# Block 1's row statistics on ScalarE, two turned quarters copied by VectorE, chunk 2's scores in one PE run, and a new order table, in an attention-plus-ReGLU layer

## The chip, the core and the metric

The kernel runs on one core of a Trainium2 chip. The metric is device microseconds of one execution, lower is better. The core has a matrix engine (TensorE; PE in the profile, with PEld for its weight loads), VectorE (DVE), ScalarE (ACT), GpSimd (POOL) and SyncE (SP). Each takes its instructions in the order in which the program lists them, and waits for the others by semaphores. SP, ACT and POOL also issue DMAs.

## The reference

Input x is 2048 rows of 512 values in bfloat16. An attention block and a gated linear block follow each other, both on normalised rows, both added to what came in:

```python
def _layernorm(x, axis=-1, eps=1e-5):
    m = jnp.mean(x, axis=axis, keepdims=True)
    v = jnp.var(x, axis=axis, keepdims=True)
    return (x - m) / jnp.sqrt(v + eps)
...
    qkv = (x @ wqkv)                     # 32 heads of 16
    idx = pos[:, None] - (arange(8) * 2) # each row sees itself and 7 rows before, 2 apart
    logits = einsum("bhsd,bhswd->bhsw", q, kg) * scale   # masked where idx < 0
    o = einsum("bhsw,bhswd->bhsd", softmax(logits), vg)
    h = x + o @ wo
...
    gate, up = n @ W_gate, n @ W_up      # n = _layernorm(h), F = 1376
    h2 = h + (gate * (gate > 0) * up) @ W_down
```

## The kernel before

The 2048 rows are worked in four chunks (tk = 0 to 3) of 512 rows, and a chunk has four blocks of 128 rows (j = 0 to 3), one row to a partition. A chunk goes through these steps:

- **Normalise x** (`layernorm`, from line 453). For a block j, VectorE makes mean and variance (BN_STATS at L488, BN_AGGR at L491), ScalarE makes 1/sqrt(var + eps) as exp(-0.5 ln(var + eps)) (L504 and L508), and the block is scaled: in chunk 0 by VectorE (L539), in chunks 1 to 3 by ScalarE (L536), which needs a small VectorE product for its bias first (nb, L512). Chunk 0 does this block by block (`XG[0]` has four groups), the others in one group of four.
- **Turn** the rows, so that features lie on partitions: PE transposes (L568) into a PSUM bank, which is copied to SBUF (L584); the fourth chunk's x and the rows of the second half are turned by DMA (L557). In chunk 0 each block is a quarter of the turned tile `quad`, with a copy of its own.
- **q, k, v** (PE L609, copied out by ScalarE at L617). In chunk 0 the first outputs are made in parts: a half-width part "a" over quarters 0 and 1, a half-width part "b" over quarters 2 and 3, then full-width parts.
- **Scores** in two halves of four neighbours each: VectorE multiplies q by shifted k (L675 in chunk 0, L660 later), PE sums over the head by a matrix of ones (`sel`, four 32-column strips side by side). In the halves named by `PRE` VectorE first adds the two products (L704), and PE's run is 8 matmuls (L718) in place of 16 (L666). ScalarE takes exp (L746). `MS = (3,)` names the chunks in which both halves' score matmuls stand in one PE run.
- **Softmax and values**: sum and reciprocal (L763, L769, L772), DMAs that spread the weights over partitions (L806), VectorE products with shifted v (L853 in chunk 0, L838 later), sums partly by accumulating DMAs (L881), output projection (PE L919), residual and row sum (DVE L930).
- **Gated block**: normalise h, turn it, gate and up (PE L996), their last 96 columns (PE L959), relu and copies on ScalarE (L1001, L1003, L1006), product on VectorE (L1027), down projection (PE L1050), and the output row (DVE L1058 in chunks 2 and 3).

The program is written by a planner. Every step is an `Op` with an engine, an estimated cost and its dependencies; `RANK` gives each one a place. `Plan.order` takes the steps strictly in the order of RANK, gives each a planned start and a buffer, and the steps are then emitted by planned start. On one engine that is the order of RANK. The estimated costs decide which buffer of a pool a step gets, and nothing else of the result.

The names that the change touches are settings ahead of `layernorm`: `MS`, `TEV` (quarters of chunk 0 whose turned copy VectorE makes), `XS` (where ScalarE makes the row statistics of x) and `RANK`. The steps it touches run through these lines:

```python
groups = XG[tk]
xnT, xev, _, _ = layernorm(tk, xload[tk], xnT_s, lnp, groups, LNA[0][tk])
...
tev = not residual and tk == 0 and j0 in TEV
if tev: V.tensor_copy(out=o, in_=i)
else:   nc.scalar.copy(out=o, in_=i)
```

Of the kernel before, what the change touches and what calls it, by code (L numbers as in the profile page):

```python
# [201 lines left out]
def kernel(  # L202
# [187 lines left out]
    BDI = {"S": 0.63, "A": 0.65, "P": 0.95}  # L390

    RPE, POW = (), ()

    MERGE = (0, 1, 2, 3)

    MS = (3,)

    BCN = 4

    HG = ([[0, 1, 2, 3]],) * 4  # L400
    HSP = ()
    XG = ([[0], [1], [2], [3]], [[0, 1, 2, 3]], [[0, 1, 2, 3]], [[0, 1, 2, 3]])
# [737 lines left out]
```

## Time and profile before

| | |
|---|---|
| median of 3 runs | 191.66 us (191.09 to 192.36) |
| the profiled execution | 191.45 us |
| span inside it | 189.7 us, so 1.75 us lie around the span |
| PE busy | 183.7 us, 97% |
| VectorE busy | 148.9 us, 79% |
| ScalarE busy | 117.2 us, 62% |
| GpSimd busy | 25.1 us, 13% |

All sums are made against the 191.45 us of the profiled execution, whose trace is the one shown; it lies 0.21 us under the median. Times in the rows count from the start of the span. A merged row of the timeline shows start, length, engine, line, operation, tiles written and read, and the count; in brackets stands how long the engine had been idle before it, and what ended that. Matmuls are pipelined: a row's length holds the tail of its last one, so the pace of PE is read from starts, not from the lengths of single matmuls.

### The profile page before, as it was taken

Reading aid. Unit: us, or ns where it says so; the run is one execution under the profiler, and the core shown is the slowest. Engines: PE = TensorE matmul, PEld = TensorE weight load, DVE = VectorE, ACT = ScalarE, POOL = GpSimd, SP = SyncE. Lnnn points to the kernel's source line nnn. Section 1 sums busy time; section 2 is a strip of 40 time slices with the busy share of each in tenths; the row PEclk is TensorE's granted clock in tenths of the full one; section 3 lists DMA queues with packets and bytes.
Section 4 is the critical chain, followed back from the end, with each engine's and each line's share of the span. In section 5 each row is a group of like instructions: output and inputs, shape, how many; then the busy total and the mean of one; then the engine's idle time right before and its main releaser. Section 6 shows DMA issues by size and latency. Waiting matters only on the chain.

```text
span 189.7 us, 2952 instructions
## 1 busy us (share of the span) xinstructions
PE 183.7 (97%) x1058; PEld 93.3 (49%) x1077; DVE 148.9 (79%) x226; ACT 117.2 (62%) x239; POOL 25.1 (13%) x47
## 2 busy tenths in 40 slices
PE   7799999999999999999999999999999999999994
PEld 7655455554444444544444554455444444455543
DVE  5799989999999999999999997999473720115343
ACT  2769999986496867925477783047465702659600
POOL 4000311500000024040031351013300000000000
PEclk9999999999999999999999999999999999999999
DMA  6999294992497869943564999666970150200313
GB/s 170 294 321 386 52 215 88 198 198 47 146 242 166 246 179 188 201 77 107 109 133 83 194 181 196 141 128 143 194 133 3 28 138 0 83 3 28 100 54 95
DMA packets 27742, 26.96 MB, mean 142 GB/s; under 512 B 14704, under 2 KB 23248, under 8 KB 27728
## 3 DMA queue, kind: packets, MB, share of 16 engines
q1 hardware_dynamic: 23552, 15.21, 29.3%
q0 software_dynamic: 3312, 10.49, 29.1%
q10 hardware_dynamic: 864, 1.08, 1.8%
q8 instruction: 8, 0.13, 0.3%
q14 instruction: 6, 0.05, 0.1%
HBM read 8.42 MB, written 2.10 MB: 55 GB/s over the span
## 4 chain that ended last, share of the span: by engine, by line
PE 79%; DVE 7%; DMA 7%; ACT 3%; issue 2%; POOL 0%; DVEq 0%
PE bank L996 36%; PE bank L1050 20%; PE bank L609 10%; PE bank L919 7%; DMA x_sm<-in_A_x_dram 4%; DVE big L675 4%; PE bank L959 3%; DMA big<-ex 3%; DVE st L488 2%; ACT row L536 2%; PE bank L666 2%; PE bank L718 1%; DVE big L853 1%; ACT quad L617 1%; POOL big L806 0%
## 5 line engine op out<-in xcount | busy, mean ns | idle before, releaser
L996 PE MATMUL bank<-quad,wgu_sb 128*128 128x512 bf16 x312 | 71.4, 379 | 0.4
L996 PEld LDWEIGHTS <-wgu_sb 128*128 128x128 bf16 x320 | 31.0, 98 | 36.9 <-issue 1.3
L1050 PE MATMUL bank<-wd_sb,gT 128*128 128x512 bf16 (+4 forms) x193 | 39.3, 355 | 0.3
L1006 ACT ACTIVATE gr<-bank 128x512 bf16<-128x512 f32 x40 | 22.9, 600 | 12.1 <-PE bank L996 7.4
L609 PE MATMUL bank<-quad,wqk_sb 128*128 128x512 bf16 (+1 forms) x130 | 29.6, 370 | 0.6 <-ACT quad L584 0.4
L1050 PEld LDWEIGHTS <-gT 128*128 128x128 bf16 (+1 forms) x198 | 18.5, 98 | 19.6
L1003 ACT CAST up_sb<-bank 128x512 bf16<-128x512 f32 x30 | 17.3, 588 | 16.5 <-PE bank L996 14.3
L1027 DVE TENSOR_TENSOR gT<-gr,up_sb 128x1024 bf16<-128x1024 bf16 x20 | 13.6, 688 | 14.8 <-ACT up_sb L1003 10.0
L660 DVE TENSOR_TENSOR big<-quad,kT 128x4096 bf16<-128x4096 bf16 x11 | 25.0, 2287 | 0.0
L609 PEld LDWEIGHTS <-wqk_sb 128*128 128x128 bf16 x134 | 14.8, 114 | 13.4 <-issue 1.9
L838 DVE TENSOR_TENSOR big<-big,vT 128x4096 bf16<-128x4096 bf16 x9 | 20.2, 2288 | 0.0
L609 PE MATMUL bank<-quad,wv_sb 128*128 128x512 bf16 x62 | 15.5, 379 | 0.1
L930 DVE SCALAR_TENSOR_TENSOR x_sm<-x_sm,bank 128x512 bf16<-128x512 bf16 x16 | 10.7, 680 | 5.6 <-PE bank L919 5.6
L1058 DVE SCALAR_TENSOR_TENSOR row<-bank,iv,x_sm 128x512 bf16<-128x512 f32 (+2 forms) x10 | 6.2, 641 | 11.3 <-ACT iv L508 7.8
L478 ACT ACTIVATE junk<-x_sm,sm 128x512 bf16<-128x512 bf16 x16 | 11.5, 724 | 5.7 <-DVE x_sm L930 5.7
L919 PE MATMUL bank<-wo_sb,quad 128*128 128x512 bf16 x64 | 15.0, 379 | 0.0
L1056 ACT ACTIVATE up_sb<-bank,iv 128x512 bf16<-128x512 f32 x8 | 5.3, 685 | 13.2 <-PE bank L1050 13.2
L881 POOL DMA_DIRECT2D big<-big x12 | 10.5, 878 | 21.6 <-DVE big L838 11.5
L841 DVE TENSOR_TENSOR big<-big 128x1024 bf16<-128x1024 bf16 (+2 forms) x18 | 11.7, 661 | 0.7 <-DMA big<-big 0.6
L488 DVE BATCH_NORM_STATS2 st<-x_sm 128x6 f32<-128x512 bf16 x16 | 10.4, 676 | 1.9 <-DMA x_sm<-in_A_x_dram 1.9
L617 ACT CAST kT<-bank 128x512 bf16<-128x512 f32 x16 | 9.1, 594 | 3.0 <-PE bank L609 3.0
L806 POOL DMA_DIRECT2D big<-ex x12 | 6.8, 591 | 26.9 <-DVE st L488 19.4
(80 smaller groups left out, 188.0 us busy)
## 6 DMA issues: line engine op xcount, KB each, us to landing
big<-big POOLq DMA_DIRECT2D x12, 512.0 KB, 5.5
big<-ex SPq DMA_DIRECT2D x20, 128.0 KB, 2.8
big<-ex POOLq DMA_DIRECT2D x12, 128.0 KB, 4.5
wqk_sb<-wqk_sb POOLq DMA_DIRECT2D x3, 512.0 KB, 5.5
wgu_sb<-in_B_W_gate_dram SPq DMA_DIRECT2D x1, 1376.0 KB, 10.4
wgu_sb<-in_B_W_up_dram SPq DMA_DIRECT2D x2, 688.0 KB, 4.9
wd_sb<-in_B_W_down_dram SPq DMA_DIRECT2D x2, 640.0 KB, 5.5
x_sm<-in_A_x_dram SPq DMA_DIRECT2D x2, 512.0 KB, 6.3
```

The source lines that it names most:

```text
L478: nc.scalar.activation(out=junk[:, j % 2, :], in_=h.t[:] if h else x_sm[:, tk * BPC + j, :], func=ACT.Square, bias=sm.t[:, j:j + 1], scale ...
L488: V.bn_stats(out=st.t[:], in_=x_sm[:, tk * BPC + j, :])
L609: nc.tensor.matmul(mm.t[:, lo:hi], lhsT=wv_sb[:, dt, t:D:NT] if c == 2 else wqk_sb[:, dt, c * D + t:(c + 1) * D:NT], rhs=xnT.t[:, dt, lo:h ...
L660: V.tensor_tensor(out=pb.t[:].rearrange("p (t w) s -> p t w s", t=2), in0=q4, in1=k4, op=ALU.mult)
L838: V.tensor_tensor(out=mt.t[:], in0=ab.t[:], in1=v8, op=ALU.mult)
L841: V.tensor_tensor(out=mt.t[:, 0:n, :], in0=mt.t[:, 0:n, :], in1=mt.t[:, n:2 * n, :], op=ALU.add)
L919: nc.tensor.matmul(od.t[:], lhsT=OT.t[:, t, j * P:(j + 1) * P], rhs=wo_sb[:, t, :], start=(t == 0), stop=(t == NT - 1 and tk not in RPE))
L996: nc.tensor.matmul(mm.t[:fs, lo:hi], lhsT=wgu_sb[:, dt, g, ft * P: ft * P + fs], rhs=hnT.t[:, dt, lo:hi], start=(dt == 0), stop=(dt == NT ...
L1003: nc.scalar.copy(out=ub.t[:fs, i, :], in_=um.t[:fs, :])
L1006: nc.scalar.activation(out=gr.t[:fs, i, :], in_=gm.t[:fs, :], func=ACT.Relu, scale=-1.0 if tk in HX else 1.0)
L1027: V.tensor_tensor(out=gt.t[:fs, 0:n, :], in0=gr.t[:fs, 0:n, :], in1=ub.t[:fs, 0:n, :], op=ALU.mult)
L1050: nc.tensor.matmul(od.t[:, c0:c1], lhsT=gts[ft].t[:fs, ft % 2, j * P:(j + 1) * P], rhs=wd_sb[:fs, ft, c0:c1], start=(ft == 0), stop=(ft == ...
```

## The change

The settings change in four places:

- `XS = ((0, 1),)`: in chunk 0 the statistics of block 1 are made by ScalarE. A Copy activation with scale -1/512 sums the row (its accumulator gives minus the mean), and a Square activation with that as bias sums the squared deviations. The setting now names pairs of chunk and group, where it named chunks. The block is then scaled on VectorE by (x + minus mean) times the reciprocal root.
- `TEV = (2, 3)`: the turned copies of quarters 2 and 3 of chunk 0 are made by VectorE.
- `MS = (2, 3)`: chunk 2's two score halves stand in one PE run, too.
- `RANK` is another table, so all engines get another order, and buffers change places. One estimated cost (the issue of chunk 0's first half of spreading DMAs on GpSimd) is 0.85 in place of 0.35.

New branches for the bias product (`f_na`, `f_n1`, `XNA`) are not reached with these settings. The arithmetic of all other steps stays as it was. Lines from 480 on move down by 6 to 16: L568 is L584 after the change, L584 is L598 (VectorE) and L600 (ScalarE), L609 is L625, L666 is L682, L718 is L734.

```diff
 RANK = [
-    1, 0, 3, 2, 4, 6, 7, 8, 9, 10, 15, 11, 16, 17, 18, 19, 20, 21, 5, 12,
...
+    1, 0, 3, 2, 6, 8, 11, 10, 15, 16, 13, 12, 17, 14, 18, 19, 20, 21, 4, 7,
...
-    MS = (3,)
+    MS = (2, 3)
...
-    TEV = ()
+    TEV = (2, 3)
     HX = (0,)
-    XS = ()
+    XS = ((0, 1),)
+    XNA = ()
...
-        own = not residual and tk in XS
-        sm, sq = (residual, Buf(sq_s)) if residual else (Buf(sm_s), Buf(sq_s)) if own else (None, None)
+        has = not residual and [g for g in groups if (tk, g[0]) in XS]
+        sm, sq = (residual, Buf(sq_s)) if residual else (Buf(sm_s), Buf(sq_s)) if has else (None, None)
...
+            own = not residual and (tk, grp[0]) in XS
...
                             nc.scalar.activation(out=junk[:, j % 2, :], in_=x_sm[:, tk * BPC + j, :],
-                                                 func=ACT.Copy, accum_out=sm.t[:, j:j + 1])
+                                                 func=ACT.Copy, scale=-1.0 / D, accum_out=sm.t[:, j:j + 1])
...
-                                             bias=sm.t[:, j:j + 1], scale=-float(D), accum_out=sq.t[:, j:j + 1])
+                                             bias=sm.t[:, j:j + 1], scale=1.0 if own else -float(D), accum_out=sq.t[:, j:j + 1])
...
                 elif own:
                     nc.scalar.activation(out=rs.t[:, lo:hi], in_=sq.t[:, lo:hi], func=ACT.Ln,
-                                         bias=eps_t[:, 0:1], scale=float(D) ** -3)
+                                         bias=eps_t[:, 0:1], scale=1.0 / D)
...
+                elif own:
+                    V.tensor_scalar(out=xn.t[:], in0=x, scalar1=sm.t[:, j:j + 1], scalar2=rs.t[:, j:j + 1], op0=ALU.add, op1=ALU.mult)
```

**ScalarE at the start of the program, before**: after the table load come the four pairs of Ln (L504) and Exp (L508) for the reciprocal roots `rs` of blocks 1, 0, 3 and 2, then the four copies of turned quarters, then the first q and k copies. `mv` holds VectorE's mean and variance.

```order
L328 ACT_TABLE_LOAD
L504 ACTIVATE rs0_131<-mv0_117,eps_t_66 128x1
L508 ACTIVATE rs0_131<-rs0_131 128x1
L504 ACTIVATE rs0_131<-mv0_117,eps_t_66 128x1 x2
L508 ACTIVATE rs0_131<-rs0_131 128x1 x2
L584 COPY quad0_79<-bank1_141 128x4x128
L584 COPY quad0_79<-bank2_142 128x4x128
L584 COPY quad0_79<-bank3_143 128x4x128
L584 COPY quad0_79<-bank4_144 128x4x128
L617 CAST kT_77<-bank1_141 128x512
```

**The same place after the change**: `sm` is minus the mean of block 1, `sq` its squared deviations. In the program's operands the Ln steps are of blocks 1, 0, 3 and 2, the Exp steps of blocks 0, 1, 3 and 2.

```order
L328 ACT_TABLE_LOAD
L478 ACTIVATE junk_139,sm0_121<-x_sm_71 128x512
L484 ACTIVATE junk_139,sq0_124<-x_sm_71,sm0_121 128x512
L507 ACTIVATE rs0_131<-sq0_124,eps_t_66 128x1
L510 ACTIVATE rs0_131<-mv0_117,eps_t_66 128x1
L514 ACTIVATE rs0_131<-rs0_131 128x1
L510 ACTIVATE rs0_131<-mv0_117,eps_t_66 128x1
L514 ACTIVATE rs0_131<-rs0_131 128x1 x2
L600 COPY quad0_79<-bank1_141 128x4x128
L600 COPY quad0_79<-bank2_142 128x4x128
L633 CAST kT_77<-bank5_145 128x512
```

Two full-row activations now stand ahead of every reciprocal root, and two of the four copies are gone from this queue.

**VectorE at the same place, before**: four blocks' statistics are done ahead of the four scaled blocks (`row0` to `row3`), and behind those stand the statistics of chunk 1.

```order
L488 BN_STATS st3_116<-x_sm_71 128x6
L491 BN_AGGR mv0_117<-st2_115 128x2
L491 BN_AGGR mv0_117<-st3_116 128x2
L539 TENSOR_SCALAR row0_104<-x_sm_71,mv0_117,rs0_131 128x512
L539 TENSOR_SCALAR row1_105<-x_sm_71,mv0_117,rs0_131 128x512
L539 TENSOR_SCALAR row2_106<-x_sm_71,mv0_117,rs0_131 128x512
L539 TENSOR_SCALAR row3_107<-x_sm_71,mv0_117,rs0_131 128x512
L488 BN_STATS st0_113<-x_sm_71 128x6
```

**VectorE there after the change**:

```order
L494 BN_STATS st2_115<-x_sm_71 128x6
L497 BN_AGGR mv0_117<-st2_115 128x2
L555 TENSOR_SCALAR row0_104<-x_sm_71,mv0_117,rs0_131 128x512
L553 TENSOR_SCALAR row1_105<-x_sm_71,sm0_121,rs0_131 128x512
L555 TENSOR_SCALAR row2_106<-x_sm_71,mv0_117,rs0_131 128x512
L555 TENSOR_SCALAR row3_107<-x_sm_71,mv0_117,rs0_131 128x512
L598 COPY quad0_79<-bank3_143 128x4x128
L598 COPY quad0_79<-bank4_144 128x4x128
L494 BN_STATS st3_116<-x_sm_71 128x6
```

One block's statistics are gone from VectorE's queue, and two copies stand between the scaled blocks and the statistics of chunk 1.

**VectorE later, between chunk 0's value products (L853), before**: `nb2` is the bias product of chunk 2's normalisation; ScalarE's scaled rows of chunk 2, and PE's transposes of them, wait for it.

```order
L491 BN_AGGR mv3_120<-st3_116 128x2
L853 TENSOR_TENSOR big0_88<-big4_92,vT_78 128x2048
L853 TENSOR_TENSOR big2_90<-big4_92,vT_78 128x2048
L853 TENSOR_TENSOR big0_88<-big4_92,vT_78 128x2048
L512 SCALAR_TENSOR_TENSOR nb2_129<-mv3_120,rs3_134 128x4
L853 TENSOR_TENSOR big1_89<-big4_92,vT_78 128x2048
```

**VectorE at that place after the change**:

```order
L869 TENSOR_TENSOR big0_88<-big4_92,vT_78 128x2048
L497 BN_AGGR mv3_120<-st0_113 128x2
L869 TENSOR_TENSOR big3_91<-big4_92,vT_78 128x2048 x2
L497 BN_AGGR mv3_120<-st1_114 128x2
L497 BN_AGGR mv3_120<-st2_115 128x2
L869 TENSOR_TENSOR big1_89<-big4_92,vT_78 128x2048 x2
L518 SCALAR_TENSOR_TENSOR nb2_129<-mv3_120,rs3_134 128x4
```

The bias product stands behind five value products, where it stood behind three. In PE's order the transposes of the block that ScalarE scales last have moved back as well: eight more 512-wide matmuls and four more transposes stand ahead of them.

More of the change, by code (lines that the diff above doesn't have):

```diff
@@ L458, in layernorm @@
         mv, rs, nb = Buf(mv_s), Buf(iv_s if residual else rs_s), Buf(nb_s)
-        own = not residual and tk in XS
-        sm, sq = (residual, Buf(sq_s)) if residual else (Buf(sm_s), Buf(sq_s)) if own else (None, None)
+        has = not residual and [g for g in groups if (tk, g[0]) in XS]
+        sm, sq = (residual, Buf(sq_s)) if residual else (Buf(sm_s), Buf(sq_s)) if has else (None, None)
+        if not residual and len(has) == len(groups):
+            mv = None
+        nact = on_act
         evs, ivd = [], []
@@ L522, in layernorm @@
             else:
-                l = add((ln + "rl" + gk, tk), "ACT", AS, f_ln, ag, pr, take=[rs], use=[sq or mv], lat=AL)
+                l = add((ln + "rl" + gk, tk), "ACT", AS, f_ln, ag, pr, take=[rs], use=[sq if residual or own else mv], lat=AL)
                 e = add((ln + "re" + gk, tk), "ACT", AS, f_ex, [l], pr, use=[rs], lat=AL)
@@ L526, in layernorm, with f_xn @@
                 ivd.append(e)
-            elif on_act and not residual:
-                e = add((ln + "nb" + gk, tk), "DVE", DSM, f_nb, [e], pr, take=[nb], use=[sm if own else mv, rs], lat=DL)
-            def f_xn(j, xn):
+            elif on_act and own and hi == lo + 1:
+                e = add((ln + "nb" + gk, tk), "ACT", AS, f_n1, [e], pr, take=[nb], use=[sm, rs], lat=AL)
+            elif on_act:
+                e = add((ln + "nb" + gk, tk), "DVE", DSM, f_na if own else f_nb, [e], pr, take=[nb], use=[sm if own else mv, rs], lat=DL)
+            def f_xn(j, xn, own=own, on_act=on_act):
                 x = x_sm[:, tk * BPC + j, :]
```

18 lines of the change are left out of this document (11 added, 7 removed), and 74 rows, old and new, of the table RANK.

## The prediction

> **What bounds the kernel now.** I read the page's first part, the chain of waits, PE's waits and the windows, in this order. The first two lines are the page's busy time of PE and the shares of the chain by engine; then the three waits that PE's own list has; then two of twenty-microsecond windows (PE, PEld, DVE, ACT, POOL busy, with counts); then pieces of the chain in order of time.
>
> ```profile
> PE 183.7 (97%) x1058; PEld 93.3 (49%) x1077; DVE 148.9 (79%) x226; ACT 117.2 (62%) x239; POOL 25.1 (13%) x47
> PE 79%; DVE 7%; DMA 7%; ACT 3%; issue 2%; POOL 0%; DVEq 0%
> ...
> PE bank L438 <- DVE warm L329: 1.0, 1, 1.0
> PE bank L568 <- DVE row L539: 0.7, 1, 0.7
> PE bank L609 <- ACT quad L584: 0.4, 2, 0.2
> ...
> 80.00:100.00 20.00, 19.89 (x96) 9.23 (x97) 19.86 (x30) 10.27 (x24) 4.00 (x6) 1.00 0.51 109
> 140.00:160.00 20.00, 19.89 (x92) 9.08 (x93) 7.88 (x20) 8.29 (x19) 0.00 (x0) 1.00 0.22 47
> ...
> 36.17 0.62 PE bank L568 x8
> 37.51 7.93 PE bank L609 x36
> 59.94 6.26 PE bank L996 x29
> 186.91 0.35 DVE row L1058
> ```
>
> PE is the bound, and it is nearly without holes. Its waits add up to 2.1 us and all fall before 9.5 us. From 37 us to the last matmul the chain is PE's, and 29 matmuls in 6.26 us give its pace: 0.216 us for one 512-wide matmul, which is also the start-to-start distance inside every longer run. VectorE is as full as PE until 100 us (19.86 of 20), but PE does not wait for it there. So the time is made of four pieces: the head until the first q and k matmuls flow, PE's own work, any new hole in it, and the tail behind the last matmul (186.91 to 189.7). An edit elsewhere is worth nothing. The granted clock is 1.00 in both windows; I see no reason for it to change.
>
> **The change part by part.**
>
> *Chunk 2's score halves in one run.* The chain's pieces of score runs, chunk 2's two and chunk 3's merged one:
>
> ```profile
> 66.85 0.98 PE bank L666 x16
> ...
> 69.45 0.55 PE bank L718 x8
> ...
> 101.21 0.98 PE bank L718 x16
> ```
>
> Sixteen matmuls take 0.98 us whether they are one half or two, eight take 0.55; so eight more cost 0.43 and a run has 0.12 us of its own. One run of 24 takes 0.98 + 0.43 = 1.41 in place of 1.53: 0.12 us less. The entry into a run costs something too: matmuls of the second run start at 69.38 where eight L959 matmuls of 0.082 us begun at 68.63 are through at 69.29, 0.09 us that are also paid once less. The gain lies between 0.12 and 0.21; I take 0.2, since both rows are of this place. What it asks for: both halves' products must be there before the one run starts. VectorE's last step for them is this:
>
> ```profile
> 63.32 2.29 DVE L704 TENSOR_TENSOR big<-big,big 128x4096 bf16<-128x4096 bf16 x1
> 66.78 1.05 PE L666 MATMUL bank<-big,sel 128*32 128x512 bf16 x16
> 68.63 0.82 PE L959 MATMUL bank<-wgu_sb,quad 128*128 128x192 bf16 x8
> 69.38 0.62 PE L718 MATMUL bank<-big,sel 128*32 128x512 bf16 x8
> ```
>
> It ends at 65.61. By the order the merged run stands one run's worth of work behind 66.78, so the products are 1 to 2 us early and cover the merge; the exps behind it come 1 us later for one half and earlier for the other, with 1 us of VectorE's queue to spare.
>
> *The head.* These rows are the timeline of the first ten microseconds, and two of ScalarE's row sums later on:
>
> ```profile
> 3.14 1.28 ACT L328 ACT_TABLE_LOAD   x1 [3.14 <-issue]
> 5.22 0.30 ACT L504 ACTIVATE rs<-mv,eps_t 128x1 f32<-128x1 f32 x1 [0.80 <-DVE mv L491]
> 5.55 0.20 ACT L508 ACTIVATE rs<-rs 128x1 f32<-128x1 f32 x1
> 6.47 0.48 ACT L504 ACTIVATE rs<-mv,eps_t 128x1 f32<-128x1 f32 x2
> 6.49 1.35 DVE L539 TENSOR_SCALAR row<-x_sm,mv,rs 128x512 bf16<-128x512 bf16 x4
> 6.93 1.37 PE L568 MATMUL bank<-identity,row 128*128 128x128 bf16 x16 [0.71 <-DVE row L539]
> 7.36 2.05 ACT L584 COPY quad<-bank 128x512 bf16<-128x512 bf16 x4 [0.17 <-PE bank L568]
> 8.49 0.82 PE L609 MATMUL bank<-quad,wqk_sb 128*128 128x256 bf16 x6 [0.19 <-ACT quad L584]
> 9.18 1.88 DVE L488 BATCH_NORM_STATS2 st<-x_sm 128x6 f32<-128x512 bf16 x3 [1.33 <-DMA x_sm<-in_A_x_dram]
> 9.47 6.43 PE L609 MATMUL bank<-quad,wqk_sb 128*128 128x256 bf16 x31 [0.16 <-ACT quad L584]
> ...
> 64.79 0.71 ACT L478 ACTIVATE junk<-x_sm,sm 128x512 bf16<-128x512 bf16 x1
> 65.40 0.19 ACT L478 ACTIVATION_READ_ACCUMULATOR junk<-x_sm,sm 128x1 f32 x1
> ...
> L841 DVE TENSOR_TENSOR big<-big 128x512 bf16<-128x512 bf16 x4 | 1.7, 425 | 0.0
> L1058 DVE SCALAR_TENSOR_TENSOR row<-bank,iv,x_sm 128x512 bf16<-128x512 f32 x7 | 5.0, 746 | 10.3 <-ACT iv L508 7.8 <-PE bank L1050 2.4
> ```
>
> A summing activation and its accumulator read take 64.79 to 65.59, 0.80 us. ScalarE is free at 4.42, after the table load. With 0.03 between dependent steps the sum of block 1 is there at 5.25, the squares at 6.08. Ln of block 1 runs at 6.11; Ln of block 0 follows 0.18 later, as in the row of two (0.48 less one 0.30), and ends at 6.59; its Exp ends at 6.82. So the first scaled block can start at 6.87, 0.38 later than the 6.49 of now. The other Exps follow, the last about 7.68, which fits VectorE's distance of 0.32 from block to block: the four start at 6.87, 7.19, 7.51, 7.83. PE's transposes shift alike, from 6.93 to 7.31, and so do ScalarE's first two copies (7.36 to 7.74 for the first). Part "a" of q and k, which waits for the second, starts at 8.87 in place of 8.49. That is the loss.
>
> Against it stands the second pair of quarters. Now ScalarE makes four copies in a row (7.36 to 9.41) and part "b" waits until 9.47; the six "a" matmuls, at half the pace of a full one (0.108), are through at 9.14. With two engines, PE ends the fourth block's transposes at 8.70 (8.30 now, 6.93 + 1.37, and 0.40 later since the fourth scaled block starts at 7.83 in place of 7.43) and the third's at 8.38, and VectorE copies them one after the other. No row shows such a copy: 0.425 (128x512 bfloat16 out of SBUF) and 0.746 (128x512 out of PSUM, one more tensor to read) are the nearest; I take 0.45, near the first, since it has one source and 16-bit data. They end at 8.83 and 9.28. Part "b" can then go at 9.3, just when the four "a" matmuls that the order puts ahead are through (8.87 + 0.43). At 9.47 PE has then done 4 + 1.6 half-width matmuls where it has done 6 now: 0.04 us behind. With 0.746 the copies end at 9.87, and PE is 0.67 behind. With the sums 0.1 shorter (the first has no bias to read) it is 0.15 ahead. VectorE's copies are covered by its idle 1.33 us ahead of 9.18, where it waits for x; at 0.45 each they pass that point by 0.1, and VectorE has next to no idle time after it. I take 0.1 us loss for the head, with -0.15 to +0.7.
>
> [...]
>
> *The new order.* The only hole that PE has behind 9.8 us is at 36.17, where a transpose waits for the block that ScalarE scales last:
>
> ```profile
> 27.65 3.50 DVE L853 TENSOR_TENSOR big<-big,vT 128x2048 bf16<-128x2048 bf16 x3 [0.53 <-DMA big<-ex]
> 31.06 0.16 DVE L512 SCALAR_TENSOR_TENSOR nb<-mv,rs 128x4 f32<-128x4 f32 x1
> 31.14 5.76 DVE L853 TENSOR_TENSOR big<-big,vT 128x2048 bf16<-128x2048 bf16 x5
> 31.26 2.22 ACT L536 ACTIVATE row<-x_sm,nb,rs 128x512 bf16<-128x512 bf16 x3 [0.32 <-DVE nb L512]
> 35.29 0.83 ACT L536 ACTIVATE row<-x_sm,nb,rs 128x512 bf16<-128x512 bf16 x1
> 35.72 0.38 PE L763 MATMUL bank<-row,spread 128*128 128x512 bf16 x1
> ```
>
> The matmul at 35.72 leaves PE free at 35.94, so the hole is 0.23. After the change the bias product stands behind two more value products of 1.14 us (five in 5.76, the last 1.22) and two aggregates: 33.5 in place of 31.06. ScalarE's four scaled blocks then run from 33.7, at 0.71 each, with three copies of 0.5 between: the last ends at 38.0. PE comes to it after eight more matmuls and four more transposes, 8 x 0.216 + 0.22 = 1.95 us behind 35.94, at 37.9. The hole is then about 0.15, as small as now. I take 0, with -0.23 (it closes) to +0.8 (the value products, which begin when a DMA lands, come 0.7 later). In the tail the last row in four pieces stands as before, in the same order on PE and VectorE. For all other moved steps I found no place where a step came later than PE's need, and I count nothing, with +0.8 for one that I missed.
>
> Sum: -0.2 + 0.1 + 0 = -0.1 on 191.45, so 191.35. I forecast 191.3, 0.2% under the median shown.
>
> **The rivals.**
>
> *ScalarE's queue holds the head back.* The two sums stand ahead of every reciprocal root, and ScalarE takes its queue in order: if the head comes out at the slow end (+0.7), VectorE's queue carries the lateness along, and PE's second score run gives nothing back: 191.45 + 0.7 - 0.2 = 191.95, slower than before. These are VectorE's products of chunk 0 and that run; the products end at 21.12 and the run starts at 21.26:
>
> ```profile
> 13.08 8.04 DVE L675 TENSOR_TENSOR big<-quad,kT 128x2048 bf16<-128x2048 bf16 x7
> 21.26 1.05 PE L666 MATMUL bank<-big,sel 128*32 128x512 bf16 x16
> ```
>
> It decides against me once VectorE's second copy ends after 9.5. For it: the 0.38 that the first block is late. Against: 1.33 us of VectorE's idle time. [...]
>
> *The new order opens holes between 21 and 45 us.* There VectorE and ScalarE run as full as PE, and the value products wait for DMAs. If the scaled blocks of chunks 2 and 3 come 1 us after PE's need, one hole of 0.8 to 1.2 follows: 192.3. For it: my own margin there is under 0.2 us. Against: the steps moved back together.
>
> *The holes close.* The hole at 36.17 goes and the head gains 0.15: 191.45 - 0.2 - 0.23 - 0.15 = 190.9.
>
> **How the numbers follow.** The forecast 0.55 (190.9 to 191.7 by its own terms), the late head 0.17, the holes 0.14, the closing 0.14. The range leaves out the ends of the outer cases: 190.5 to 192.6; the runs themselves scatter from 191.09 to 192.36. What can be told from no change is about 1%, 1.9 us. No case reaches that on either side: 0.04 for faster, since all of PE's holes together hold under 1 us; 0.06 for slower, two of the losses together with one that I don't see; 0.90 for the same.
>
> **What would show it.** In the profile after: one run of 24 score matmuls of about 1.4 us near 68 us; the first scaled block near 6.9, the first q or k matmul near 8.9 and no wait of PE at 9.5; VectorE copies of 0.4 to 0.5 us ending before 9.4; PE's waits none behind 10 us but small ones near 38. The forecast is wrong if PE shows a wait of over 0.5 us behind 10 us, if the last matmul lies over 1 us from where it is now, or if the tail behind it has changed.

## The result and the profile after

The changed kernel takes 193.05 us (median of 17 executions, 192.04 to 196.97), the kernel before 191.67 in the same series: a ratio of 1.0073, 95% interval 1.0054 to 1.0091. It is slower by 0.7%. The prediction, 191.3 with a range to 192.6, lay on the other side of the kernel before, and the measured time lies above that range.

Each execution also has a mean granted clock of TensorE. An execution over 1.5% above the fastest of its kernel counts as disturbed and is left out of the ratios and of the counts of the clock, here and below, but not of the medians. Of the changed kernel's executions in this series and in a second one below, 12 of 25 undisturbed ones had a clock of 0.990 or 0.991, the others 0.998 to 1.000; of the kernel before, in the series of the experiments, 1 of 121 was that low. The profiled execution, 192.12 us, is one at 1.000 and lies near the lower end. So it can't show what the low clock costs.

First the page's busy time and chain shares by engine, then PE's whole list of waits, then pieces of the chain in order of time (start, length, what), then PE rows of the timeline; all of the changed kernel's profiled execution, span 190.3 us:

```profile
PE 183.5 (96%) x1058; PEld 93.4 (49%) x1077; DVE 149.8 (79%) x226; ACT 117.4 (62%) x241; POOL 25.2 (13%) x47
PE 64%; DVE 14%; DMA 9%; issue 4%; SPq 3%; ACT 3%; ACTq 1%; POOL 0%; POOLq 0%; DVEq 0%
...
PE bank L584 <- DVE row L555: 1.1, 1, 1.1
PE bank L439 <- DVE warm L329: 1.0, 1, 1.0
PE bank L625 <- DMA quad<-row: 0.5, 1, 0.5
PE bank L625 <- ACT quad L600: 0.2, 1, 0.2
...
30.56 3.17 DMA quad<-row
95.18 3.30 DMA big<-ex
98.70 2.29 DVE big L854
111.01 0.35 DVE row L794
111.40 0.39 PE bank L779
187.56 0.35 DVE row L1074
...
33.78 1.06 PE L625 MATMUL bank<-quad,wv_sb 128*128 128x512 bf16 x4 [0.55 <-DMA quad<-row]
68.27 1.05 PE L682 MATMUL bank<-big,sel 128*32 128x512 bf16 x16
69.14 0.60 PE L734 MATMUL bank<-big,sel 128*32 128x512 bf16 x8
```

PE's own work is 0.2 us shorter, and chunk 2's 24 score matmuls stand in one run (L682 and L734, 68.27 to about 69.7). Two things are new. PE waits 0.55 us at 33.78 for chunk 3's DMA-turned rows. And from 60 to 111 us the chain no longer runs on PE: PE's share fell from 79% to 64%, and it goes through a transfer that lands at 98.48, VectorE's value product at 98.70 and VectorE's sum of chunk 3's exponents (L794), which ends at 111.35, just ahead of the denominator matmul at 111.40. VectorE's row behind the last matmul starts 0.65 us later than before (187.56 against 186.91), and the tail behind it is the same within 0.1 us. The hole at 36.17 has gone.

The head's rows, VectorE and PE:

```profile
6.84 0.41 DVE L555 TENSOR_SCALAR row<-x_sm,mv,rs 128x512 bf16<-128x512 bf16 x1 [0.88 <-ACT rs L514]
7.30 1.36 PE L584 MATMUL bank<-identity,row 128*128 128x128 bf16 x16 [1.08 <-DVE row L555]
8.38 0.76 DVE L598 COPY quad<-bank 128x512 bf16<-128x512 bf16 x2 [0.17 <-PE bank L584]
8.86 0.81 PE L625 MATMUL bank<-quad,wqk_sb 128*128 128x256 bf16 x6 [0.19 <-ACT quad L600]
```

PE stands idle 1.08 us ahead of its first transposes, where it was 0.71. That is the only trace here of what the first experiment is about.

### The profile page after: what moved, and what is told of

Its sections match the earlier page's. It is cut to its first block, busy times and chain, and to the rows that moved or that the text cites. A ratio compares the mean times of both kernels' runs of the same rounds, so it can differ in the third digit from the quotient of the medians.

```text
span 190.3 us, 2959 instructions
## 1 busy us (share of the span) xinstructions
PE 183.5 (96%) x1058; PEld 93.4 (49%) x1077; DVE 149.8 (79%) x226; ACT 117.4 (62%) x241; POOL 25.2 (13%) x47
## 3 DMA queue, kind: packets, MB, share of 16 engines
q10 hardware_dynamic: 864, 1.08, 1.8%
## 4 chain that ended last, share of the span: by engine, by line
PE 64%; DVE 14%; DMA 9%; issue 4%; SPq 3%; ACT 3%; ACTq 1%; POOL 0%; POOLq 0%; DVEq 0%
PE bank L625 19%; PE bank L1012 19%; PE bank L1066 15%; PE bank L935 5%; DVE big L854 4%; DMA big<-big 3%; SPq L822 3%; DMA wd_sb<-in_B_W_down_dram 2%; PE bank L975 2%; DMA big<-ex 2%; DMA quad<-row 2%; PE bank L682 2%; DVE x_sm L946 1%; PE bank L584 1%; DVE big L676 1%
## 5 line engine op out<-in xcount | busy, mean ns | idle before, releaser
L1066 PE MATMUL bank<-wd_sb,gT 128*128 128x512 bf16 (+3 forms) x195 | 39.4, 355 | 0.2
L625 PE MATMUL bank<-quad,wqk_sb 128*128 128x512 bf16 (+1 forms) x130 | 29.4, 369 | 0.4 <-ACT quad L600 0.2
L1019 ACT CAST up_sb<-bank 128x512 bf16<-128x512 f32 x30 | 17.0, 597 | 15.5 <-PE bank L1012 10.9
L1043 DVE TENSOR_TENSOR gT<-gr,up_sb 128x1024 bf16<-128x1024 bf16 x20 | 13.7, 687 | 13.1 <-ACT gr L1022 10.5
L854 DVE TENSOR_TENSOR big<-big,vT 128x4096 bf16<-128x4096 bf16 x10 | 22.6, 2287 | 0.2 <-DMA big<-ex 0.2
L625 PEld LDWEIGHTS <-wqk_sb 128*128 128x128 bf16 x134 | 15.0, 113 | 12.2 <-issue 0.3
L897 POOL DMA_DIRECT2D big<-big x13 | 11.9, 916 | 63.2 <-PE bank L682 32.1
L625 PE MATMUL bank<-quad,wv_sb 128*128 128x512 bf16 x63 | 16.3, 380 | 0.7 <-DMA quad<-row 0.5
L484 ACT ACTIVATE junk<-x_sm,sm 128x512 bf16<-128x512 bf16 x17 | 12.4, 729 | 5.1 <-DVE x_sm L946 4.9
L935 PE MATMUL bank<-wo_sb,quad 128*128 128x512 bf16 x62 | 14.7, 379 | 0.1
L857 DVE TENSOR_TENSOR big<-big 128x1024 bf16<-128x1024 bf16 (+2 forms) x19 | 12.4, 659 | 1.9 <-DMA big<-big 1.8
L625 PEld LDWEIGHTS <-wv_sb 128*128 128x128 bf16 x64 | 6.9, 114 | 7.7 <-issue 1.3
```

Source lines behind the costliest of these rows:

```text
L484: nc.scalar.activation(out=junk[:, j % 2, :], in_=h.t[:] if h else x_sm[:, tk * BPC + j, :], func=ACT.Square, bias=sm.t[:, j:j + 1], scale ...
L625: nc.tensor.matmul(mm.t[:, lo:hi], lhsT=wv_sb[:, dt, t:D:NT] if c == 2 else wqk_sb[:, dt, c * D + t:(c + 1) * D:NT], rhs=xnT.t[:, dt, lo:h ...
L854: V.tensor_tensor(out=mt.t[:], in0=ab.t[:], in1=v8, op=ALU.mult)
L935: nc.tensor.matmul(od.t[:], lhsT=OT.t[:, t, j * P:(j + 1) * P], rhs=wo_sb[:, t, :], start=(t == 0), stop=(t == NT - 1 and tk not in RPE))
L1019: nc.scalar.copy(out=ub.t[:fs, i, :], in_=um.t[:fs, :])
L1043: V.tensor_tensor(out=gt.t[:fs, 0:n, :], in0=gr.t[:fs, 0:n, :], in1=ub.t[:fs, 0:n, :], op=ALU.mult)
```

## The experiments

Eighteen runs, each timed against the kernel before on its chip (there 191.53, 191.70, 191.62, 191.66 and 191.66 us, chip by chip). "Clock low" counts the executions at 0.990 or 0.991.

| run | median us | ratio to before, 95% | clock low |
|---|---|---|---|
| head_only | 192.86 | 1.0077 (1.0051 to 1.0103) | 6 of 6 |
| order_only | 192.32 | 1.0041 (1.0018 to 1.0064) | 1 of 12 |
| after_warm | 192.58 | 1.0060 (1.0037 to 1.0083) | 0 of 6 |
| before_cool | 191.59 | 1.0012 (0.9994 to 1.0030) | 3 of 12 |
| es_early | 192.13 | 1.0026 (1.0010 to 1.0042) | 0 of 12 |
| rows_early | 191.90 | 1.0007 (0.9984 to 1.0031) | 0 of 12 |
| both_early | 192.07 | 1.0015 (0.9993 to 1.0037) | 0 of 12 |
| head_warm | 191.29 | 0.9975 (0.9951 to 1.0000) | 0 of 12 |
| after_again | 193.41 | 1.0088 (1.0061 to 1.0115) | 5 of 9 |
| mu_late | 193.07 | 1.0081 (1.0058 to 1.0105) | 0 of 6 |
| all_three | 193.15 | 1.0086 (1.0065 to 1.0108) | 0 of 6 |
| head_merge_warm | 191.14 | 0.9982 (0.9965 to 0.9999) | 0 of 12 |
| early_new | 194.00 | 1.0120 (1.0092 to 1.0148) | 0 of 6 |
| late_new | 193.82 | 1.0111 (1.0085 to 1.0138) | 0 of 6 |
| after_warm_again | 192.11 | 1.0027 (1.0011 to 1.0043) | 0 of 12 |
| merge_only | 191.21 | 0.9990 (0.9970 to 1.0010) | 0 of 12 |
| new_less | 192.29 | 1.0028 (1.0015 to 1.0040) | 0 of 10 |
| old_less | 190.96 | 0.9966 (0.9953 to 0.9978) | 0 of 9 |

after_warm and after_warm_again are the same kernel on two chips, 0.47 us apart. So differences of under half a microsecond between runs of different chips are not read.

### 1. The clock: is it the longer hole in the head?

The head alone, on the order of the kernel before (the table of ranks is rebuilt so that only the head's operations take the new order):

```diff
-    XS = ()
+    XS = ((0, 1),)
-    TEV = ()
+    TEV = (2, 3)
```

> The change's head alone (block 1's row statistics on ScalarE, the two quarters copied by VectorE, the head's order as in the changed kernel); behind the head the order of the kernel before, chunk 2's scores in two runs. Clock theory (the longer TensorE hole ahead of the first transposes, 1.08 us where it was 0.71, lets some executions stay at half clock for a stretch longer): about half of the executions show a mean granted clock near 0.99, those come out near 192.6, the others near 191.6, the median 0.4 to 0.9 us above the kernel before. Order theory (what is lost comes from the new order behind 21 us): the time of the kernel before within 0.2 us, clock 1.0 in all executions. No wait for DMA-turned rows at 33.8 us under either.

192.86, and all six executions have the low clock, where half were expected. The same head with a warm-up that bridges the hole (after_warm has this edit on the changed kernel):

```diff
-    NWARM, NFILL = (62, 15), (0, 0, 0)
+    NWARM, NFILL = (62, 33), (0, 0, 0)
```

> The head of the change alone, as in the run of the head alone (192.86, all executions at a mean granted clock of 0.991), with the longer warm-up. Clock theory: clock 1.0 in all executions and the time of the kernel before within 0.2 us, 191.4 to 191.7. If the head costs something beside the clock (ScalarE's queue): 192 or more at clock 1.0.

> The changed kernel with 18 more warm-up matmuls of 128 columns (33 for 15), so that TensorE's hole ahead of the first transposes goes from 1.08 us to about 0.1 us; nothing else changes. Clock theory: no execution below a mean granted clock of 0.999, median 0.4 to 0.8 us below the changed kernel's 193.05: 192.2 to 192.7, the profiled wait at 33.8 us stays. Order theory: clock as before and no change: 193.0.

head_warm comes to 191.29 and none of its executions has the low clock: with this warm-up the head costs nothing that can be measured. What the longer warm-up does to the kernel before was not run, so a small price of the head could hide behind a gain of the warm-up. These are windows (start:end, length, busy of PE, PEld, DVE, ACT and POOL with counts, granted clock, DMA share, GB/s) and PE rows, first of head_only, then of head_warm:

```profile
7.30:8.80 1.50, 1.37 (x16) 0.97 (x17) 1.33 (x5) 1.37 (x4) 0.00 (x0) 1.00 1.00 355
8.80:10.80 2.00, 1.72 (x8) 1.24 (x9) 2.00 (x5) 0.01 (x1) 0.00 (x0) 0.51 1.05 340
10.60:12.30 1.70, 1.57 (x5) 0.68 (x5) 1.20 (x6) 0.47 (x1) 0.00 (x0) 0.51 0.93 259
12.30:14.00 1.70, 1.70 (x11) 1.05 (x10) 0.43 (x1) 1.10 (x4) 0.00 (x0) 1.00 1.00 343
...
4.95 0.96 PE L439 MATMUL bank<-warm 128*128 128x128 bf16 x10
7.30 1.37 PE L584 MATMUL bank<-identity,row 128*128 128x128 bf16 x16 [1.40 <-DVE row L555]
```
```profile
8.80:10.80 2.00, 1.73 (x12) 1.32 (x12) 2.00 (x5) 0.34 (x2) 0.00 (x0) 1.00 0.87 256
...
4.95 2.74 PE L439 MATMUL bank<-warm 128*128 128x128 bf16 x28
7.52 1.15 PE L584 MATMUL bank<-identity,row 128*128 128x128 bf16 x16
```

The expectation had one point the wrong way round: it took the clock to be low before the hole and to stay so for longer. In head_only's profile it is 1.00 in every window from the start to 8.8 us, in the pause and at the transposes from 7.30 on, too. It falls behind them, to 0.51, from 8.8 to 12.3 us, and PE does 8 matmuls in two microseconds where head_warm does 12. A mean of 0.991 over 191.2 us is 1.7 us of lost clock, or 3.5 us at 0.51, as long as that stretch. The pause of 1.40 us and the 16 transposes stand between the last warm-up matmul and the fall; why it comes only behind the transposes, and what sets its length, no run shows. The pause is not the same in every execution, since the warm-up does not always end at the same time: the 13 warm-up matmuls from 4.63 us on take 1.59 us in the changed kernel's second profile and 1.03 in that of merge_only. The latter, below, has the head of the kernel before; it shows a pause of 1.27 where the kernel before shows 0.71, and its clock stays at 1.0:

```profile
6.93 1.37 PE L568 MATMUL bank<-identity,row 128*128 128x128 bf16 x16 [1.27 <-DVE row L539]
```

The change starts the transposes at 7.30 in place of 6.93 and leaves the warm-up as it is. So it should add about 0.37 us to the pause, whatever it was.

> The kernel before with 4 fewer warm-up matmuls of 128 columns (11 for 15), so that TensorE's hole ahead of the first transposes goes from 0.71 us to about 1.14 us, as long as in the changed kernel; nothing else changes. Clock theory: about half of the executions or more show a mean granted clock near 0.99, median 0.4 to 0.9 us above the kernel before. Order theory: no change, within 0.2 us.

With four warm-up matmuls fewer (11 for 15), the kernel before has the low clock in 3 of 12 executions, at 192.22 against 191.43 for the other nine. So a warm-up that ends earlier, and the longer hole with it, brings the low clock about with none of the change in place, though more rarely than expected. Its profile has a pause of 1.30 us with the clock at 1.0. That execution took 192.57 at full clock; PE waits 1.52 us in it for a DMA-turned tile, until 128.77, so the old order has late transfers in some executions, too.

> The changed kernel once more, on the same chip as the three below, as their base. From its first timing: 193.05 (192.6 to 193.4), about half of the executions at a mean granted clock near 0.99 and those 0.5 to 0.9 us above the others. If the clock's stretch is a matter of one chip: no execution near 0.99.

The changed kernel again has it in 5 of 9 executions. In its first series the low executions have a median of 193.46 and the others 192.74; in the second 193.45 and 192.89. With the longer warm-up it takes 192.58 and 192.11. On half of the executions the clock costs 0.6 to 0.7 us, about 0.3 on the mean. The changed head on the old order pays 1.6 us (192.86 against 191.29, two chips), the kernel before with the shorter warm-up 0.8 (192.22 against 191.43, one chip). So the price is not set by the order alone; what sets it is not shown, and neither profile of the changed kernel holds an execution with the low clock.

### 2. Head, merge and order apart

> The kernel before with one edit: chunk 2's two score halves in one TensorE run, the rest of the order, the head and the warm-up untouched. As priced in the prediction: 0.12 to 0.21 us of TensorE's work gone, 191.3 to 191.5 where the kernel before gives 191.6. If the first half's scores, which now wait for the second half's sum, hold up chunk 2's exponents: no gain or up to 0.5 us slower.

> The new order behind the head and chunk 2's scores in one run, with the head of the kernel before (statistics on VectorE, quarters copied by ScalarE). Order theory: the 0.50 us wait at 33.8 us for chunk 3's DMA-turned rows is there, about 0.5 to 0.7 us above the kernel before less 0.2 for the one run of scores: 192.0 to 192.4, clock 1.0 in all executions. Clock theory: no execution near 0.99, and so 0.5 us or more below the changed kernel's median of 193.05. If the whole loss is the order's: 193.

> The changed head and chunk 2's scores in one run, with the order of the kernel before behind the head, and the longer warm-up: the change without its new order. The run of the head alone on this warm-up gave 191.29; the one run of scores takes 0.2 us of TensorE's work away: 191.1 (190.9 to 191.3), a little faster than the kernel before. If the merge costs waits instead (the first half's scores now wait for the second half's sum): 191.4 to 191.8.

The edit of merge_only; its table of ranks is rebuilt so that on PE the four matmuls of L996 and eight of L959 that stood between the two runs now stand ahead of the one run, and the other engines keep their order:

```diff
-    MS = (3,)
+    MS = (2, 3)
```

Chunk 2's merge alone gives 191.21 against 191.66 on its chip: the interval of the ratio holds the 0.2 us that the prediction gave it, and no change. Head, merge and long warm-up on the old order give 191.14; the same three on the new order are after_warm, 192.58 and 192.11. So the order by itself, with the buffer places that go with it, costs 1.0 to 1.4 us. order_only says the same from the other side: old head, clock low in one execution of 12, and 192.32, 1.1 above the merge alone. All but one of its executions lie between 191.2 and 192.9, and its profiled one, 191.21, shows no wait at 33.8 or at 111 us: the order's waits come in some executions and not in others.

### 3. Where in the order: three moves

On the changed kernel with the longer warm-up, one instruction of VectorE is moved:

```diff
 L1043 TENSOR_TENSOR gT<-gr,up_sb 128x1024
 L854 TENSOR_TENSOR big<-big,vT 128x4096
+L794 TENSOR_TENSOR row<-ex,ex 128x512
 L1043 TENSOR_TENSOR gT<-gr,up_sb 128x1024
 L854 TENSOR_TENSOR wqk_sb<-big,vT 128x4096
-L794 TENSOR_TENSOR row<-ex,ex 128x512
```

or two of ScalarE:

```diff
+L550 ACTIVATE row<-x_sm,nb,rs 128x512
+L550 ACTIVATE row<-x_sm,nb,rs 128x512
 L785 ACTIVATE bank<-bank 128x512
 L633 CAST quad<-bank 128x512
-L550 ACTIVATE row<-x_sm,nb,rs 128x512
-L550 ACTIVATE row<-x_sm,nb,rs 128x512
```

> The changed kernel with the longer warm-up (33 matmuls), so that TensorE's clock is out of the question, and with one VectorE instruction moved: chunk 3's sum of the two exponent tiles (L794) stands one silu-gate product and one value product (0.6 + 2.2 us) earlier in VectorE's queue. Theory A (chunk 3's denominator at 111 us waits for that sum; 0.18 us in the changed kernel's profile, 0.70 in that of the longer warm-up): no wait at 111 us, 0.4 to 0.7 us below the longer warm-up's 192.58, about 192.0. Theory B (chunk 3's DMA-turned rows at 33.8 us are the loss): unchanged, 192.6.

> The changed kernel with the longer warm-up and, on ScalarE, chunk 3's third and fourth scaled rows put back ahead of the logarithm L785 and one quarter copy, as in the kernel before, so that the DMA transposes can be issued earlier. Theory B (those rows are the loss): no wait at 33.8 us, 0.3 to 0.5 us below the longer warm-up's 192.58, about 192.2; the spread of the executions narrows. Theory A (the sum at 111 us is the loss): unchanged, 192.6.

> The changed kernel with the longer warm-up and both moves (chunk 3's sum earlier on VectorE, chunk 3's scaled rows earlier on ScalarE). If the two waits and the clock are the whole loss: the kernel before less the 0.2 us of the one run of scores, 191.3 (191.1 to 191.6). If the new order loses elsewhere too (38.6 us): 191.8 to 192.1.

192.13, 191.90 and 192.07, on one chip. The two moves together are no faster than either, and neither stands clear of 192.11, the better of the two base runs. The wait at 33.8 us is in none of the profiles with the longer warm-up, so what the move of the rows does cannot be read there. The executions of rows_early do lie closer together, as its theory had it (11 of 12 from 191.47 to 192.03), but those of both_early, with the same move, spread from 191.60 to 192.47. Of the sum's move it can: the wait goes from 111 us and another stands 7 us further on. Here is PE around 111 us in after_warm, then in es_early, and what PE and VectorE wait for at 117 us in es_early:

```profile
111.91 0.39 PE L779 MATMUL bank<-row,same 128*128 128x512 bf16 x1 [0.53 <-DVE row L794]
```
```profile
111.12 0.38 PE L779 MATMUL bank<-row,same 128*128 128x512 bf16 x1
118.16 2.12 PE L935 MATMUL bank<-wo_sb,quad 128*128 128x512 bf16 x9 [0.16 <-DVE quad L891]
116.95 0.69 DVE L857 TENSOR_TENSOR wqk_sb<-wqk_sb 128x1024 bf16<-128x1024 bf16 x1 [0.42 <-DMA wqk_sb<-wqk_sb]
```

The denominator waits no more; chunk 2's output projection (L935) does, for VectorE, which waits for an accumulating DMA. The third move puts the value product that waits at 98.70 back behind chunk 3's last score sum:

```diff
-L854 TENSOR_TENSOR big<-big,vT 128x4096
 L720 TENSOR_TENSOR wqk_sb<-wqk_sb,big 128x4096
+L854 TENSOR_TENSOR big<-big,vT 128x4096
```

> The changed kernel with the longer warm-up, and chunk 2's first value product (L854, the one that starts at 98.70 us and waits for the broadcast DMAs) put back behind chunk 3's last score sum (L720), as in the kernel before. Theory C (VectorE stands still there for a DMA, 0.25 to 0.85 us in the profiles of the new order, and all of its later work to 118 us moves by as much; the sum at 111 us and the projections at 118 us only show it): 0.4 to 0.7 us below the changed kernel with the longer warm-up, 191.9 to 192.2 where that was 192.58, no VectorE wait near 99 us. Theory A (the sum's own place in the queue): less than 0.2 us gained, the wait at 111 us stays.

> The changed kernel with the longer warm-up and all three moves: chunk 3's scaled rows earlier on ScalarE, chunk 3's sum earlier and chunk 2's first value product later on VectorE. If these hold the order's whole loss (theories A, B and C together): 191.1 to 191.4, level with the head alone on the longer warm-up (191.29) or 0.2 us below it by the one run of scores. If the new order also leaves VectorE too late elsewhere: 191.8 to 192.1, as with the first and the second move alone.

193.07, which is 0.5 to 1.0 above the two base runs, and 193.15, which is 1.1 above both_early: worse, against every theory. VectorE's wait near 99 us is gone, and this is what stands at 118 us in mu_late:

```profile
118.05 0.69 DVE L857 TENSOR_TENSOR wqk_sb<-wqk_sb 128x1024 bf16<-128x1024 bf16 x1 [2.08 <-DMA wqk_sb<-wqk_sb]
119.26 1.04 PE L935 MATMUL bank<-wo_sb,quad 128*128 128x512 bf16 x4 [1.54 <-DVE quad L891]
```

The product that was moved back feeds the first of four accumulating DMAs, which is now issued at 102.93. All of VectorE's later work to 111 us came earlier (the sum starts at 110.36, in after_warm at 111.44), and nothing was gained by it: theory C, as it was put, falls. That a late product at 99 us costs nothing does not follow, since this run takes the wait away by starting the product later still, at 100.35.

### 4. The order in two halves

> The changed head with the longer warm-up and chunk 2's scores in one run; the new order only for the stretch up to chunk 2's first products (about 10 to 55 us), behind it the order of the kernel before. Theory V (VectorE is the next engine behind TensorE from 60 to 118 us, and the new order of that late stretch takes its slack): 191.1 to 191.4, level with the old order throughout (191.14), the waits of the early stretch costing at most 0.3. Theory B (chunk 3's DMA-turned rows at 33.8 us and the rest of the early stretch are the loss): about 192.

> The other half: the order of the kernel before up to about 55 us, the new order behind it; head, warm-up and one run of scores as in the run beside it. Theory V: the loss is here, 191.8 to 192.6, with a TensorE wait at 111 us (the sum of chunk 3's exponents) or at 118 us (chunk 2's output projection). Theory B: 191.1 to 191.4 and no such wait.

> The changed kernel with the longer warm-up once more, beside the two halves of its order on the same chip: 192.58 as before (192.3 to 192.9), clock 1.0 in all executions. If the two halves' losses add up, its distance from 191.14 (about 1.4 us) is the sum of theirs; if one half's waits cover the other's, less than the sum.

Both halves are slower than the whole, 194.00 and 193.82, so they do not divide its loss. Where the two orders meet, VectorE stands idle in both, first early_new, then late_new:

```profile
58.12 0.76 DVE L806 TENSOR_TENSOR ex<-ex,rec 128x512 bf16<-128x512 bf16 x2 [2.31 <-ACT rec L788]
57.95 0.76 DVE L806 TENSOR_TENSOR ex<-ex,rec 128x512 bf16<-128x512 bf16 x2 [2.10 <-ACT rec L788]
```

Their medians say nothing about the theories. Their rows say one thing: late_new, with the old order up to 55 us, has the wait at the denominator (113.15) and VectorE's wait for the transfer ahead of the value product:

```profile
113.15 0.39 PE L779 MATMUL bank<-row,same 128*128 128x512 bf16 x1 [0.51 <-DVE row L794]
100.46 2.29 DVE L854 TENSOR_TENSOR big<-big,vT 128x4096 bf16<-128x4096 bf16 x1 [0.73 <-DMA big<-ex]
```

early_new has neither. So in these two profiles the pair of waits goes with the late stretch of the new order, and not with what stands ahead of it.

### 5. VectorE's slack, or the DMAs?

A part of chunk 3's second score sum is left out, in the new order and in the old one (both with the new head, the merge and the long warm-up); nothing is moved:

```diff
-                    V.tensor_tensor(out=p0.t[:], in0=p0.t[:], in1=p1.t[:], op=ALU.add)
+                    V.tensor_tensor(out=p0.t[:, 0:w, :], in0=p0.t[:, 0:w, :], in1=p1.t[:, 0:w, :], op=ALU.add)
```

with w = 4 for that one sum and 8 for the others.

> The changed kernel with the longer warm-up, with a part of the computation left out: chunk 3's second-half score sum (L720) adds one half of its width, so VectorE has 1.1 us less to do at about 101 us; order and every other instruction are the same. Theory V (in the new order VectorE's late stretch has no slack, and its lateness is what TensorE waits for at 111 and 118 us): no such wait, 0.5 to 0.8 us below the same kernel with the whole sum (192.58 and 192.11 on two chips): 191.3 to 191.8. If VectorE is not what bounds there (DMA landings alone, or waits spread over the early stretch): 192.0 or more, a wait at 111 or 118 us stays.

> The control: the same part of the sum left out in the changed head with chunk 2's one run of scores and the longer warm-up, on the order of the kernel before (191.14 with the whole sum). Theory V: VectorE has slack there (the sum of chunk 3's exponents stands 6 us ahead of its reader), so 1.1 us less work moves nothing: 191.0 to 191.3. If VectorE bounds the late stretch in both orders: 190.3 to 190.7.

192.29 and 190.96. The new order gains nothing from 1.1 us less on VectorE. Nor does the old one, where the sum is early anyhow (4.2 us by the rows quoted further down, not the 6 of the expectation). In new_less's profile the wait at the denominator is gone, and PE and VectorE wait 7 us later:

```profile
117.15 0.69 DVE L857 TENSOR_TENSOR wqk_sb<-wqk_sb 128x1024 bf16<-128x1024 bf16 x1 [1.20 <-DMA wqk_sb<-wqk_sb]
118.36 1.90 PE L935 MATMUL bank<-wo_sb,quad 128*128 128x512 bf16 x7 [0.42 <-DVE quad L891]
```

So VectorE's slack, taken alone, is not the bound there either. These are GpSimd's DMA issues (start, length, line, tiles), first in the kernel before, then in new_less; below each stand a window (columns as above) and single transfers with size and time from issue to landing:

```profile
98.41 0.86 POOL L1079 DMA_DIRECT2D x_sm<-up_sb  x1 [2.83 <-ACT up_sb L1056]
102.40 0.85 POOL L881 DMA_DIRECT2D big<-big  x1 [3.13 <-DVE big L838]
110.62 0.84 POOL L881 DMA_DIRECT2D big<-big  x1 [2.03 <-DVE big L838]
104.00:110.00 6.00, 6.00 (x35) 3.09 (x33) 6.00 (x6) 4.22 (x8) 1.68 (x2) 1.00 1.00 188
x_sm<-up_sb POOLq DMA_DIRECT2D x1, 256.0 KB, 3.3
big<-big POOLq DMA_DIRECT2D x1, 512.0 KB, 5.2
```
```profile
101.68 0.86 POOL L897 DMA_DIRECT2D big<-big  x1 [4.01 <-DVE big L854]
102.24 1.18 POOL L1095 DMA_DIRECT2D x_sm<-up_sb  x1
110.63 0.84 POOL L897 DMA_DIRECT2D wqk_sb<-wqk_sb  x1 [1.96 <-DVE wqk_sb L854]
104.00:110.00 6.00, 6.00 (x40) 2.62 (x41) 6.00 (x5) 4.24 (x9) 1.68 (x2) 1.00 1.04 190
wqk_sb<-wqk_sb POOLq DMA_DIRECT2D x1, 512.0 KB, 6.5
```

Before, the second residual transfer (x_sm<-up_sb, 256 KB) is issued at 98.41 and through in 3.3 us, ahead of the first value accumulation at 102.40. In the new order it is issued behind the first value accumulation, and it shares the DMA engines with the four, 512 KB each, at a share of 1.0 (the column ahead of GB/s). In the changed kernel's own profile it stands there too and takes 5.6 us:

```profile
101.30 0.86 POOL L897 DMA_DIRECT2D big<-big  x1 [3.50 <-DVE big L854]
101.85 1.18 POOL L1095 DMA_DIRECT2D x_sm<-up_sb  x1
x_sm<-up_sb POOLq DMA_DIRECT2D x1, 256.0 KB, 5.6
```

The last of the four, issued at 110.6 in both, takes 5.2 us before and 6.5 us in new_less, and so lands at 115.8 and 117.1. The product that it waits for can come earlier without the transfer landing earlier (in the changed kernel it is issued at 111.30 and lands at 116.3). That fits es_early, both_early, mu_late, all_three and new_less: whichever of the two paths to PE is made shorter (VectorE's sum for the denominator at 111 us, the accumulated values for the projection at 118 us), the other is as late. The times agree with it: from the issue of the first accumulation to the landing of the last it takes 13.1 to 13.4 us where the residual transfer is ahead of them (before, head_merge_warm, old_less), and 14.8 to 15.5 where it is among them, whether the four are issued within 10.0 us (the changed kernel) or within 7.8 (mu_late). At the 188 GB/s of before's window above, 256 KB take 1.4 us, an estimate that covers most of the difference.

The residual transfer is not enough to make PE wait, though. In the changed kernel's second profile (191.51) it is issued behind the first accumulation as well, at 101.23, and PE waits neither at 111 nor at 118 us; order_only's (191.21) is the same in this. In both the first value product starts without a wait for its own DMA, before 98.1, and so all four accumulations are earlier; in the profiles of the new order with a wait there, it starts at 98.70 or later. These rows are of the changed kernel's second profile:

```profile
98.08 2.29 DVE L854 TENSOR_TENSOR big<-big,vT 128x4096 bf16<-128x4096 bf16 x1
100.67 0.86 POOL L897 DMA_DIRECT2D big<-big  x1 [3.22 <-DVE big L854]
```

All this is read from the profiles; no run moved the residual transfer alone, or brought the first product's DMA in earlier, so that these are the cause stays open. How much of the 1.0 to 1.4 us lies there, and how much in waits of the early stretch, such as the 0.55 us at 33.78 in the changed kernel's profile, stays open too: the profile of one execution holds only that execution's waits.

head_merge_warm stands below both kernels: 191.14, a ratio of 0.9982 (0.9965 to 0.9999) to the kernel before. What it has beyond the merge gains nothing that can be told: merge_only stands at 191.21.

## Why the prediction was wrong, step by step

- **The head: right.** First scaled block 6.84 (6.87 predicted), transposes 7.30 (7.31), part "a" 8.86 (8.87), and no wait of PE ahead of part "b". The two VectorE copies last 0.42 us each, ending at 9.14; the price taken was 0.45.

```profile
L598 DVE COPY quad<-bank 128x512 bf16<-128x512 bf16 x2 | 0.8, 421 | 0.2 <-PE bank L584 0.2
```

  Predicted: 0.1 us lost. Measured, with the clock out of the way: 191.14 against 191.21 without this head (and with the shorter warm-up), no difference that can be told.
- **The merge: right as far as can be told.** -0.2 predicted; the median of the run of it alone is 0.45 below the kernel before, and its ratio says 0.2 below, with an interval from 0.6 below to 0.2 above.
- **"The granted clock is 1.00 in both windows; I see no reason for it to change": this step failed.** The windows quoted were at 80 and 140 us, and the place where it changes is 8.8 us (1.00 ahead of it and 0.51 behind it in head_only's profile). The prediction itself moved the first transposes by 0.38 and so lengthened PE's hole to 1.08 us, and it priced that as work that starts later, never as idle time that could lower the clock. About 0.3 us on the mean; in half of the executions 0.6 to 0.7.
- **"The new order ... I take 0": this step failed by size.** 1.0 to 1.4 us, above the 0.8 of its upper end. The one hole it looked at did close in the profiled execution, at the other end of its range (-0.23). Two things were left out of the sum. The DMA transposes of chunk 3: the rows that feed them moved on ScalarE behind L785 and a copy, and PE waits 0.55 us for them. And VectorE: "as full as PE until 100 us, but PE does not wait for it there" was true of the old order alone, where the sum of chunk 3's exponents ends 4.2 us ahead of its reader (rows of the kernel before):

```profile
104.23 0.42 DVE L778 TENSOR_TENSOR row<-ex,ex 128x512 bf16<-128x512 bf16 x1
108.84 0.38 PE L763 MATMUL bank<-row,same 128*128 128x512 bf16 x1
```

  In the new order the same sum ends 0.05 ahead of it, and with the longer warm-up PE waits 0.53 and 0.62 us for it in the two profiles. Where that wait is taken away, another stands at 118 us, for the accumulating DMAs (section 5). So the path through VectorE and the DMAs was priced at nothing; which part of it sets the time stays open.
- **The rivals.** ScalarE's queue did not hold the head back. "The new order opens holes between 21 and 45 us" came nearest, with 192.3 for a median of 193.05: it named a late block of ScalarE's and a price of 0.8 to 1.2, and the profile has a late transposed block and 0.55. But the two profiles of the changed kernel with the longer warm-up have their largest wait behind 10 us at 111 us instead, and the clock comes on top. The hole at 36 us closed without a gain in the total.
- **What was to show it wrong did:** a PE wait of 0.55 us at 33.78, over the 0.5 named.
- **What can be told.** The prediction took 1% as the least; 17 executions of each kernel give an interval of 0.2% to either side.
- **The sum, again, with what the runs give:** merge -0.2 to -0.45, head 0, order +1.0 to +1.4, clock +0.3. That is 0.85 to 1.5, and 1.4 was measured.

## What to carry to other kernels

When an edit delays TensorE's first work behind the warm-up, count the idle time that it opens as a price of its own: here 0.4 us more of it brought the low clock (0.51 from 8.8 to 12.3 us in head_only's profile) into half of the executions, 12 of 25, and with 18 more warm-up matmuls none of 18 had it. In a new order, look for the engine and the queue that are next behind the bound one and compare how far each of their products is ahead of its reader, before and after. A margin that falls from 4.2 us to 0.05 leaves nothing for a transfer that lands late: other profiles of the same order show 0.5 to 0.6 us of waiting there. And take several executions: the low clock shows in half of them, and the profiled one was among the best.

## What was not expected of the hardware

- The granted clock falls to 0.51 for 3.5 us (8.8 to 12.3) behind a pause of TensorE of 1.40 us, and the transposes right behind the pause, from 7.30, still run at 1.00 (head_only). Pauses of 1.27 and 1.30 us had no such effect in the profiles of merge_only and before_cool. Where between them the bound lies, or whether it is one, no run tells.
- Four accumulating DMAs of 512 KB, issued 2.2 to 4.4 us apart, keep the DMA engines at a share of 0.99 to 1.04 at 183 to 194 GB/s (from 104 to 110 us, in before, the changed kernel, old_less and new_less); the last of them, issued at 110.63 in new_less, took 6.5 us, and issued at 111.30 in the changed kernel 5.0, so the earlier one landed later.
